# Regrouping the seven-product stages of a three-layer kernel: six groups of 768 tokens become four of 1024 and one of 512

## The chip, the core and the metric

The kernel runs on one core of one Trainium2 chip. The metric is the device time of one execution in microseconds (us); the time before is the median of three runs. A core has a matrix engine (TensorE, "PE" in the profile, with its weight loads in a row of their own, "PEld"), three elementwise engines (VectorE "DVE", ScalarE "ACT", GpSimd "POOL"), and SyncE ("SP"), whose queue issues most of the DMA transfers. Matrix products land in PSUM, which has eight banks; one bank holds 512 float32 columns. GpSimd works on SBUF tiles alone.

## The reference

```python
# attention inside chunks of 64 tokens: q, k, v are (8, 8, 576, 64)
scores = scale * np.matmul(q_c, k_c.transpose(0, 1, 2, 4, 3))
attn = softmax(scores)                          # with 1e-09 added to the sum
x = np.matmul(attn, v_c)                        # -> (4608 tokens, 512)
# first layer pair
gate = 1.0 / (1.0 + np.exp(-(x @ w_gate)))      # 512 -> 1536
y = (gate * (x @ w_val)) @ w_out                # 1536 -> 512
# second layer pair
h = y @ w_in                                    # 512 -> 2048
g = np.where(h >= 1, h, np.where(h <= -1, 0.0, (h + 1) ** 2 / 4))
out = g @ w_out2                                # 2048 -> 512
```

## The kernel before

The work is in four parts, one after the other.

- **Projection.** Nine blocks of 512 tokens go through attention and the two products of the first pair. The products are those of `proj_part`, named `pr` in the profile, with a moving operand of 512 columns. The eight first blocks hold the first 512 tokens of each of the eight batches; one more block, `REST`, holds the last 64 tokens of all eight. The gated result `sg` goes to DRAM (`gT`, `gR`). Beside this the weights of the later parts are combined and stored.
- **Stage o** (1536 to 512), **stage i** (512 to 2048) and **stage p** (2048 to 512). Each is a matrix product in blocks that uses seven half-size products instead of eight, numbered 1 to 7 and run in the order `PO = [1, 5, 6, 2, 7, 3, 4]`. A group of tokens is cut into two halves of `N` columns; the operand of a product is a quarter of the input (`b11` to `b22`) or a difference of quarters.

Each operand is split into a high part, rounded to the matrix engine's float32 format, and a low part, the remainder. So one block product takes three matrix instructions (`three`, lines 480 to 482: high by high, high by low, low by high). An operand is made in up to three steps, and here is who does each before the change:

- `op_sub` (line 525) subtracts two quarters, in place, for products 5, 6, 7 and 4: VectorE in o and p, GpSimd in most of i;
- `op_hi` (line 529) copies the high part: ScalarE;
- `op_lo` (line 536) subtracts the high part from the source: in o and p VectorE and GpSimd in turn, in i GpSimd.

A **step** is six matrix instructions. In `down` (stages o and p) it is one slice k of one product for both halves m of the output rows; in `up` (stage i) it is one product for one m, over both slices. The order on every engine is written out by step: `on(t, prio, fn, ...)` puts a piece of work ahead of step t. `op_sub` stands 8 steps, `op_hi` 7 and `op_lo` 6 ahead of the step that uses them. `result` (lines 551 and 553) takes a finished product out of its bank: ScalarE copies products 1, 6, 5 and 4, VectorE adds 2, 7 and 3 to what is already there. Products 1, 6, 7 and 4 pile up in one bank, of which there are two sets; line 543 takes them in turn by the parity of the group (in i of the output pair).

Behind stage i stands the function g. Before the change ScalarE forms relu(h/2 + 1/2), VectorE takes the minimum with 1 and squares in one instruction (`u_square`, line 715), and VectorE takes the maximum with h (`u_join`, line 720).

There are 6 groups of 768 tokens with N = 384, so 42, 56 and 56 steps for one group in o, i and p, and 5544 matrix instructions in the three stages. In p the operands lie in 10 tiles used in a ring (`p_tile`); the weights of a stage stay in SBUF for all groups. The output leaves through a 32 by 32 transpose on VectorE (`out_store`, line 786) and DMAs with rows of 128 bytes.

```python
eng = nc.vector if turn[0] % 2 == 0 else nc.gpsimd      # op_lo, line 535
i = (14 * (NG - 1) + np_[0] % 10) % NY                  # p_tile, line 770
n = 6 * par if BANK[p] == 0 else 2 * BANK[p]            # product, line 543
```

Of the kernel before, what the change touches and what calls it, by code (L numbers as in the profile page):

```python
# [30 lines left out]
def kernel(  # L31
# [29 lines left out]
    N = 384  # L61
    GT = 2 * N
    NG = NT // GT
    NR = 28
    PO = [1, 5, 6, 2, 7, 3, 4]

    wp = ctx.enter_context(tc.tile_pool(name="wp", bufs=NR))
    cp = ctx.enter_context(tc.tile_pool(name="cp", bufs=1))
# [5 lines left out]
    yT = [dp.tile([DM, GT], F32, name=f"yT{g}") for g in range(NG)]  # L74
    uT = [dp.tile([F2 * P, GT], F32, name=f"uT{g}") for g in range(NG)]

# [19 lines left out]
    def w_load(key):  # L96
        kind, f = key
        sl = slice(f * P, (f + 1) * P)
        if kind in "gv" and keys.index(key) < 8:
            raw = wp.tile([P, 512], I64, tag="w", name="raw")  # L100
        else:
            raw = pool["raw"].tile([P, 512], I64, tag="raw", name="raw", bufs=pool["nraw"])
# [58 lines left out]
    def s_split(kind, k, part):  # L161
# [9 lines left out]
        st = pool["raw"].tile([P, 2, 2, 256], F32R, tag="raw", name="st", bufs=pool["nraw"])  # L171
# [37 lines left out]
    pool = {}  # L209
    X = {}  # L210
# [9 lines left out]
    def x_tile(n=BS, name="x"):  # L220
        return pool["x"].tile([P, 2, n], F32R, tag="x", name=name, bufs=8)
# [11 lines left out]
    class Whole:  # L233
# [162 lines left out]
        def x(self, p):  # L396
            t = X[self.b, p] = x_tile()
            for r, b in enumerate(self.B["o", p]):
                nc.scalar.activation(self.half(t, 0, r), b, AF.Copy)

        def half(self, t, i, r):
            return t[:, i].rearrange("e (g r q) -> e g r q", r=2, q=CH)[:, :, r]

        def l(self, p):
            t = X[self.b, p]
            for r, b in enumerate(self.B.pop(("o", p))):
                nc.vector.tensor_tensor(
                    out=self.half(t, 1, r), in0=b, in1=f32(self.half(t, 0, r)), op=ALU.subtract
                )

    def first_block():
# [12 lines left out]
        z = pool["sg"].tile([P, BS], F32R, tag="sg", name="z", bufs=4)  # L424
# [82 lines left out]
    turn = [0]  # L507
# [3 lines left out]
    def quarters(p, key):  # L511
        b0, b1 = B0[key], B1.get(key)
        b21, b22 = (b1[:, :N], b1[:, N:]) if b1 is not None else (None, None)
        return b0[:, :N], b0[:, N:], b21, b22

# [11 lines left out]
    def op_hi(p, key, name, tile_):  # L527
        OP[name] = o = tile_()
        nc.scalar.activation(o[:, 0], op_src(p, key), AF.Copy)  # L529

    def op_lo(p, key, name, eng=None):
        o = OP[name]
        if eng is None:
            turn[0] += 1
            eng = nc.vector if turn[0] % 2 == 0 else nc.gpsimd
        eng.tensor_tensor(out=o[:, 1], in0=op_src(p, key), in1=f32(o[:, 0]), op=ALU.subtract)  # L536

    def product(p, m, pairs, par):

        for first, args in pairs:  # L540
            first = first and p in (1, 2, 5)
            if first:
                n = 6 * par if BANK[p] == 0 else 2 * BANK[p]
                banks[BANK[p], m] = ps.tile([P, N], F32, tag=f"b{n + m}", name=f"P{BANK[p]}")
# [22 lines left out]
    def down(kind, nk, tile_, load0, load1, done, first=0):  # L567
# [407 lines left out]
```

## Time and profile before

| | us |
|---|---|
| median of 3 runs | 1660.26 (1657.21 to 1660.83) |
| the profiled execution | 1659.88 |
| its span (first to last instruction of the program) | 1658.1 |
| TensorE busy | 1636.3 (99%) |
| VectorE busy | 1154.2 (70%) |
| ScalarE busy | 853.7 (51%) |
| GpSimd busy | 720.9 (43%) |

The span begins at 0. The projection ends and stage o begins at 687.64 us; stage i begins at about 950, stage p at about 1299; the last matrix instruction begins at 1653.61. A matrix instruction's duration in the profile is longer than the distance to the next one, since instructions overlap in the array; distances between starts are what counts for the total. The same holds for VectorE, where an instruction may start before the one ahead has fully ended: a row that joins two (x2) shows it.

### The profile page before, as it was taken

The numbers are of one execution on the slowest core, as the hardware profiler recorded it, in microseconds if no ns is written. First come the engines' busy times: TensorE is split into PE (matmuls) and PEld (weight loads), VectorE is DVE, ScalarE is ACT, GpSimd is POOL, SyncE is SP. The second block draws the span as 40 slices with busy tenths as digits, with TensorE's granted clock in tenths as the row PEclk, the third lists the DMA queues.
The fourth block names the chain that finished last, engine by engine and source line by source line (L and its number), as shares of the span: only waits on it lengthen the run. The fifth ranks groups of instructions, "written<-read, shape, count | busy, mean of one in ns | idle before, by whom it ended". The sixth has DMA issues, their size and how long they took to land.

```text
span 1658.1 us, 29812 instructions
## 1 busy us (share of the span) xinstructions
PE 1636.3 (99%) x10688; PEld 1512.4 (91%) x10688; DVE 1154.2 (70%) x1833; ACT 853.7 (51%) x1566; POOL 720.9 (43%) x666
## 2 busy tenths in 40 slices
PE   7999999999999999999999999999999999999999
PEld 6778888887888888899999999999999999999998
DVE  6865555555455531487777778788787899889887
ACT  6664445444554431355555565565554555555553
POOL 2433434343444420255555564353450555555553
PEclk9999999999999999999999999999999999999999
DMA  7957777777777858355744654423328844554462
GB/s 204 268 127 206 217 211 202 209 232 232 206 220 228 236 191 327 123 153 176 218 134 134 240 217 153 153 112 143 137 115 339 324 147 113 148 164 108 111 190 39
DMA packets 399844, 307.13 MB, mean 185 GB/s; under 512 B 275920, under 2 KB 322000, under 8 KB 399696
## 3 DMA queue, kind: packets, MB, share of 16 engines
q1 hardware_dynamic: 396496, 304.84, 59.8%
q8 instruction: 84, 1.38, 0.3%
q10 hardware_dynamic: 3200, 0.39, 0.1%
q14 instruction: 64, 0.52, 0.1%
HBM read 179.83 MB, written 125.30 MB: 184 GB/s over the span
## 4 chain that ended last, share of the span: by engine, by line
PE 88%; DVE 5%; DMA 2%; SPq 2%; ACT 1%; issue 1%; POOL 1%; POOLq 0%; DVEq 0%; ACTq 0%
PE P L481 18%; PE P L482 18%; PE P L480 18%; PE pr L480 10%; PE pr L482 10%; PE pr L481 10%; PE O L390 1%; DVE z L525 1%; SPq L298 1%; PE S L342 1%; PE PT L378 1%; DMA vd<-in_v_dram 1%; DVE raw L128 1%; SPq L287 1%; DVE z L536 1%
## 5 line engine op out<-in xcount | busy, mean ns | idle before, releaser
L481 PE MATMUL P<-z,w 128*128 128x384 f32 x1344 | 450.1, 335 | 2.4 <-DVE z L536 2.1
L482 PE MATMUL P<-z,w 128*128 128x384 f32 x1344 | 449.7, 335 | 0.0
L480 PE MATMUL P<-z,w 128*128 128x384 f32 x1344 | 449.6, 335 | 0.0
L536 POOL TENSOR_TENSOR z<-z 128x384 fp32r<-128x384 f32 x256 | 290.6, 1146 | 362.4 <-ACT z L529 355.1
L480 PE MATMUL pr<-x,w 128*128 128x512 f32 x864 | 344.6, 399 | 0.0
L482 PE MATMUL pr<-x,w 128*128 128x512 f32 x864 | 337.7, 391 | 0.7 <-POOL w L138 0.7
L481 PE MATMUL pr<-x,w 128*128 128x512 f32 x864 | 337.0, 390 | 0.0
L529 ACT ACTIVATE z<-z 128x384 fp32r<-128x384 f32 x420 | 211.6, 522 | 167.5 <-DVE z L525 71.7
L930 DVE TENSOR_TENSOR sg<-pr,sg 128x512 f32<-128x512 f32 x108 | 74.5, 689 | 286.9 <-PE pr L482 120.4
L481 PEld LDWEIGHTS P<-z,w 128*128 128x128 f32 x1344 | 252.8, 188 | 3.8 <-DVE z L536 3.1
L480 PEld LDWEIGHTS P<-z,w 128*128 128x128 f32 x1344 | 252.9, 188 | 0.0
L482 PEld LDWEIGHTS P<-z,w 128*128 128x128 f32 x1344 | 252.7, 188 | 0.0
L536 POOL TENSOR_TENSOR op<-in,op 128x384 fp32r<-128x384 f32 x126 | 142.1, 1133 | 197.1 <-ACT op L529 196.0
L482 PEld LDWEIGHTS pr<-x,w 128*128 128x128 f32 x864 | 162.4, 188 | 36.4 <-POOL w L138 1.5
L480 PEld LDWEIGHTS pr<-x,w 128*128 128x128 f32 x864 | 162.4, 188 | 34.0
L481 PEld LDWEIGHTS pr<-x,w 128*128 128x128 f32 x864 | 162.7, 188 | 31.8
L927 ACT ACTIVATE sg<-pr 128x512 f32<-128x512 f32 x108 | 64.5, 597 | 236.0 <-PE pr L482 224.6
L529 ACT ACTIVATE op<-in 128x384 fp32r<-128x384 f32 x252 | 128.5, 524 | 110.9 <-DVE in L525 53.8
L525 DVE TENSOR_TENSOR z<-z 128x384 f32<-128x384 f32 x198 | 179.2, 933 | 4.2 <-POOL z L536 4.0
L482 PE MATMUL P<-op,w 128*128 128x384 f32 x504 | 168.3, 334 | 0.0
L480 PE MATMUL P<-op,w 128*128 128x384 f32 x504 | 168.3, 334 | 0.0
L481 PE MATMUL P<-op,w 128*128 128x384 f32 x504 | 168.3, 334 | 0.0
(62 smaller groups left out, 2188.6 us busy)
## 6 DMA issues: line engine op xcount, KB each, us to landing
uT<-ua SPq DMA_DIRECT2D x96, 384.0 KB, 2.3
z<-uT SPq DMA_DIRECT2D x96, 384.0 KB, 5.9
gT<-sg SPq DMA_DIRECT2D x96, 256.0 KB, 4.6
in<-gT SPq DMA_DIRECT2D x48, 384.0 KB, 4.4
raw<-in_moe_w_out_dram SPq DMA_DIRECT2D x28, 512.0 KB, 5.8
w<-swi SPq DMA_DIRECT2D x28, 512.0 KB, 6.2
w<-swp SPq DMA_DIRECT2D x28, 512.0 KB, 7.1
swi<-st SPq DMA_DIRECT2D x24, 512.0 KB, 4.2
```

The costliest lines, as they stand in the source:

```text
L128: nc.vector.scalar_tensor_tensor(out=word(1, I32), in0=word(1, I32), scalar=3, in1=word(0, I32), op0=ALU.logical_shift_left, op1=ALU.bitwi ...
L287: nc.sync.dma_start(out=t[:, i, js, h], in_=rows[h ^ u].rearrange("(j i) d -> i j d", i=P)[:, js],)
L298: nc.sync.dma_start(out=t[32 * g:32 * g + 32, i, u * step // 32:(u + 1) * step // 32], in_=part.rearrange("(t i) r -> i t r", i=32),)
L342: nc.tensor.matmul(banks[h ^ u][hs, c], lhsT=t[rows, 0, ts], rhs=t[rows, 1, ts], start=True, stop=True)
L480: nc.tensor.matmul(o, lhsT=ah, rhs=bh, start=first, stop=False, skip_group_check=open_)
L481: nc.tensor.matmul(o, lhsT=ah, rhs=bl, start=False, stop=False, skip_group_check=open_)
L482: nc.tensor.matmul(o, lhsT=al, rhs=bh, start=False, stop=stop and last, skip_group_check=open_)
L525: (eng or nc.vector).tensor_tensor(out=op_src(p, key), in0=x, in1=y, op=ALU.subtract)
L529: nc.scalar.activation(o[:, 0], op_src(p, key), AF.Copy)
L536: eng.tensor_tensor(out=o[:, 1], in0=op_src(p, key), in1=f32(o[:, 0]), op=ALU.subtract)
L927: nc.scalar.activation(sg, go, AF.Sigmoid)
L930: nc.vector.tensor_tensor(out=sg, in0=vo, in1=sg, op=ALU.mult)
```

## The change

- **Groups.** N is 512 and a group has 1024 tokens: four groups (`FULL`) of two batches' first 512 tokens, and one (`REMNANT`) of the 512 tokens of the block `REST`, with halves of 256 columns. Stages o and i run them in the order 0, 1, remnant, 2, 3 (`AMID`); stage p runs 0 to 3 and then the remnant (`LAST`). The number of steps of a group stays, so the three stages have 4620 matrix instructions: 3696 with 512 columns and 924 with 256.
- **Memory.** One pool `wp` of 46 tiles of 4 KB takes the place of the pools for weights, raw weights, x, operands, inputs and outputs. Beside it are a pool of 7 tiles (`v`) for results and values of g, and one of 4 half tiles (`hp`). The remnant puts two slices into one tile (`part`). In p, of the operands after the 32nd, three of five go to the `v` pool.
- **Weights of stage i.** The 14 odd ones of 28 are loaded again for each group (`STREAM`), 16 steps ahead.
- **Low parts.** In o and p VectorE makes them all, but for the first product of p's first group; in i GpSimd goes on, but VectorE makes the operands (differences and low parts) of the group that follows the remnant.
- **The function g.** VectorE clips h to [-1, 1] (`tensor_scalar` with max and min), ScalarE forms the square of h/2 + 1/2, VectorE joins as before.
- **Output.** The four DMAs of a transposed tile are spread over steps instead of issued together, and all stand on SyncE's queue; the results of o and p are held in tiles of one half each.

```diff
-    N = 384
-    GT = 2 * N
-    NG = NT // GT
-    NR = 28
+    N = 512
+    FULL, REMNANT = NB // 2, NB // 2
+    NG = FULL + 1
+    AMID = [*range(FULL // 2), REMNANT, *range(FULL // 2, FULL)]
+    LAST = [*range(FULL), REMNANT]
+    NR = 46
+    def cols(g):
+        return N // 2 if g == REMNANT else N
...
+            if label == "op" and kind == "p":
+                turn[0] += 1
+                if turn[0] > VOP and turn[0] % 5 < 3:
+                    return v_tile(s, dt, label)
+            return wp.tile(s, dt, tag="w", name=label)
...
         if eng is None:
-            turn[0] += 1
-            eng = nc.vector if turn[0] % 2 == 0 else nc.gpsimd
+            eng = nc.vector
...
+    def clip(dst, src):
+        nc.vector.tensor_scalar(out=dst, in0=src, scalar1=-1.0, scalar2=1.0, op0=ALU.max, op1=ALU.min)
...
     def u_square(h, m):
         u = U[h, m]
-        nc.vector.scalar_tensor_tensor(out=u, in0=u, scalar=1.0, in1=u, op0=ALU.min, op1=ALU.mult)
+        nc.scalar.activation(u, u, AF.Square, scale=0.5, bias=half)
...
+    STREAM, AHEAD = {"i": range(1, 28, 2), "p": ()}, 16
```

VectorE in the last stage, a full group, while products 6 and 7 are made ready; `z` (before) and `op`, `u` (after) are operand and input tiles, L525 and L556 the differences, L536 and L566 the low parts. Before:

```order
L536 TENSOR_TENSOR z<-z 128x384
L525 TENSOR_TENSOR z<-z 128x384 x2
L536 TENSOR_TENSOR z<-z 128x384
L525 TENSOR_TENSOR z<-z 128x384 x2
L536 TENSOR_TENSOR z<-z 128x384
```

After:

```order
L566 TENSOR_TENSOR op<-u,op 128x512
L556 TENSOR_TENSOR u<-u 128x512
L566 TENSOR_TENSOR op<-u,op 128x512
L556 TENSOR_TENSOR u<-u 128x512
L566 TENSOR_TENSOR op<-u,op 128x512
```

One low part now goes with each difference, where one went with two.

VectorE in the middle stage, one pair of output rows m of a full group, from the last added result on; `R` are results, `P` the bank, `ua` the values of g. Before:

```order
L553 TENSOR_TENSOR R_12952<-P_12969,R_12952 128x384
L715 SCALAR_TENSOR_TENSOR ua<-ua 128x768
L720 TENSOR_TENSOR ua<-R_12937,ua 128x768
L715 SCALAR_TENSOR_TENSOR ua<-ua 128x768 x2
L720 TENSOR_TENSOR ua<-R_12952,ua 128x768
L720 TENSOR_TENSOR ua<-P_12930,ua 128x384
L720 TENSOR_TENSOR ua<-R_12964,ua 128x384
L715 SCALAR_TENSOR_TENSOR ua<-ua 128x768
```

After:

```order
L583 TENSOR_TENSOR R_11624<-P_11641,R_11624 128x512
L691 TENSOR_SCALAR ua<-R_11636 128x512
L691 TENSOR_SCALAR ua<-R_11609 128x1024
L691 TENSOR_SCALAR ua<-P_11602 128x512
L691 TENSOR_SCALAR ua<-R_11648 128x512
L691 TENSOR_SCALAR ua<-R_11624 128x1024
L691 TENSOR_SCALAR ua<-P_11617 128x512
L717 TENSOR_TENSOR ua<-R_11609,ua 128x1024
L717 TENSOR_TENSOR ua<-R_11624,ua 128x1024
```

The squares have left VectorE, and clips of one source have come, all ahead of the joins.

TensorE where stage o turns into stage i, with what each instruction waits for; `P0` are banks (the number tells them apart), `op` and `z` operands, `w` weights. Before:

```order
L481 MATMUL P0_9680<-op_10053,w_7251 128x384 [waits DVE_49]
L482 MATMUL P0_9680<-op_10053,w_7251 128x384
L480 MATMUL P0_9684<-op_10053,w_7251 128x384
L481 MATMUL P0_9684<-op_10053,w_7251 128x384
L482 MATMUL P0_9684<-op_10053,w_7251 128x384
L480 MATMUL P0_10160<-z_10082,w_8304 128x384 [waits DMAHW5_49,Activation_49]
```

After:

```order
L494 MATMUL P0_9161<-op_9546,w_7231 128x512 [waits DVE_49]
L495 MATMUL P0_9161<-op_9546,w_7231 128x512
L493 MATMUL P0_9165<-op_9546,w_7231 128x512
L494 MATMUL P0_9165<-op_9546,w_7231 128x512
L495 MATMUL P0_9165<-op_9546,w_7231 128x512
L493 MATMUL P0_9636<-op_9575,w_8699 128x512 [waits DMAHW5_49,Activation_49]
```

The last row is the first product of stage i. Its wait for ScalarE was for its operand alone. By the parity of line 543 the last group of o, the fifth in the order now and the sixth before, has the set of banks that i's first pair takes (P0_9161 and P0_9636 are one bank), so the wait now covers ScalarE's copy out of P0_9161 too, whose last product ended four instructions earlier.

## Rows read from the trace of the kernel before

**Rows 1.** The page: span, busy time by engine, the chain that ended last.
```profile
span 1658.1 us, 29812 instructions
PE 1636.3 (99%) x10688; PEld 1512.4 (91%) x10688; DVE 1154.2 (70%) x1833; ACT 853.7 (51%) x1566; POOL 720.9 (43%) x666
PE 88%; DVE 5%; DMA 2%; SPq 2%; ACT 1%; issue 1%; POOL 1%; POOLq 0%; DVEq 0%; ACTq 0%
```

**Rows 2.** Timeline, TensorE (start, length): 28 instructions of 512 columns, 25 of 384.
```profile
640.04 0.39 PE L480 MATMUL pr<-x,w 128*128 128x512 f32 x1
...
646.16 0.39 PE L480 MATMUL pr<-x,w 128*128 128x512 f32 x1
...
999.67 0.33 PE L480 MATMUL P<-z,w 128*128 128x384 f32 x1
...
1003.83 0.33 PE L480 MATMUL P<-z,w 128*128 128x384 f32 x1
```

**Rows 3.** Timeline, weight loads and matrix instructions behind a break in the projection.
```profile
301.36 0.19 PEld L480 LDWEIGHTS pr<-x,w 128*128 128x128 f32 x1
301.47 0.19 PEld L481 LDWEIGHTS pr<-x,w 128*128 128x128 f32 x1
...
301.36 0.50 PE L480 MATMUL pr<-x,w 128*128 128x512 f32 x1
301.70 0.39 PE L481 MATMUL pr<-x,w 128*128 128x512 f32 x1
```

**Rows 4.** Timeline, TensorE: first and last instruction of the three stages.
```profile
687.64 0.33 PE L480 MATMUL P<-op,w 128*128 128x384 f32 x1
...
1653.61 0.34 PE L482 MATMUL P<-z,w 128*128 128x384 f32 x1
1653.98 0.58 DVE L786 STREAM_TRANSPOSE RT<-P 128x384 f32<-128x384 f32 x1 [3.58 <-PE P L482]
```

**Rows 5.** Stretches where stage p begins: busy us (and instructions), granted clock, DMA.
```profile
1250.00:1308.00 58.00, 57.84 (x334) 57.52 (x332) 44.26 (x61) 28.63 (x52) 13.84 (x11) 1.00 0.91 343
1307.00:1316.00 9.00, 7.18 (x31) 6.55 (x31) 8.97 (x14) 3.46 (x8) 3.68 (x4) 0.81 0.91 344
```

**Rows 6.** Timeline there: two waits of TensorE, and VectorE between them.
```profile
1308.16 0.44 PE L481 MATMUL P<-z,w 128*128 128x384 f32 x1 [0.32 <-POOL z L536]
1309.90 0.55 DVE L525 TENSOR_TENSOR z<-z 128x384 f32<-128x384 f32 x1
1310.37 0.55 DVE L536 TENSOR_TENSOR z<-z 128x384 fp32r<-128x384 f32 x1
1310.97 0.46 PE L481 MATMUL P<-z,w 128*128 128x384 f32 x1 [1.50 <-DVE z L536]
```

**Rows 7.** Stage p by line: duration ns min/median/max; GpSimd makes 159 low parts beside these.
```profile
L536 DVE TENSOR_TENSOR z<-z x157: 507/546/1386, 1314.8 to 1639.1; 128x384 fp32r<-128x384 f32 x157
L525 DVE TENSOR_TENSOR z<-z x184: 508/890/1408, 1315.3 to 1638.6; 128x384 f32<-128x384 f32 x184
```

**Rows 8.** Timeline, VectorE: two instructions in a row, of 256 and of 512 columns.
```profile
101.38 0.75 DVE L407 TENSOR_TENSOR x<-O,x 128x256 fp32r<-128x256 f32 x2
135.97 1.28 DVE L128 SCALAR_TENSOR_TENSOR raw<-raw 128x512 int32<-128x512 int32 x2
```

**Rows 9.** Groups by line and shape (count, busy us, mean ns): 256 and 512 columns.
```profile
L407 DVE TENSOR_TENSOR x<-O,x 128x256 fp32r<-128x256 f32 x72 | 26.9, 415 | 4.1 <-ACT x L399 4.0
L930 DVE TENSOR_TENSOR sg<-pr,sg 128x512 f32<-128x512 f32 x108 | 74.5, 689 | 286.9 <-PE pr L482 120.4 <-issue 106.9 <-ACT st L172 37.5
L927 ACT ACTIVATE sg<-pr 128x512 f32<-128x512 f32 x108 | 64.5, 597 | 236.0 <-PE pr L482 224.6 <-DMA in<-gT 4.8 <-DMA qk<-in_q_dram 2.9
L172 ACT ACTIVATE st<-raw 128x512 fp32r<-128x512 f32 x66 | 41.4, 664 | 13.4 <-POOL raw L151 6.8 <-POOL raw L153 5.3 <-DMA swp<-st 1.3
```

**Rows 10.** Stretches of stages i and p: VectorE busy is the third number.
```profile
960.00:1290.00 330.00, 330.00 (x1905) 330.00 (x1904) 267.89 (x363) 183.90 (x343) 128.18 (x111) 1.00 0.46 175
1315.00:1640.00 325.00, 324.44 (x1870) 323.64 (x1869) 295.14 (x415) 177.16 (x364) 179.08 (x159) 1.00 0.48 139
```

## What the change was predicted to do

> **What bounds the kernel now.** First the page: TensorE is busy 99% of the span and holds 88% of the chain that ended last, VectorE 5% [rows 1]. Then TensorE's first and last instruction of the three stages: 687.64 to 1653.61 and one more distance, 966.1 us [rows 4]. The change leaves the projection's work as it is, so the whole argument is about these 966.1 us. Two things can shorten them: less time from start to start, and fewer waits.
>
> The distance from start to start comes from the timeline [rows 2]. In stretches without a wait, 24 distances of 384 columns take 1003.83 - 999.67 = 4.16 us, 0.1733 each; 27 of 512 columns take 646.16 - 640.04 = 6.12 us, 0.2267 each. The 128 columns between them cost 0.0534, the clock's upper level (2.4 GHz); the granted clock of stages i and p is 1.00 [rows 10]. So an instruction pays 4 x 0.0534 for 512 columns and 0.0131 whatever its size. The columns of all instructions together stay (5544 x 384 = 3696 x 512 + 924 x 256), so fixed parts are all that the new sizes save.
>
> The waits: 5544 x 0.1733 = 960.8, so all waits before come to 966.1 - 960.8 = 5.3 us. They stand where stage p begins: from 1307 to 1316 TensorE starts 31 instructions where about 52 would fit, at a granted clock of 0.81, and VectorE is busy 8.97 of the 9 us [rows 5]. The instruction rows there say "POOL" for one wait and VectorE for a longer one of 1.50 us, with VectorE going from a difference to a low part between them [rows 6].
>
> **Instructions.** After the change 3696 x 0.2267 = 837.9. For 256 columns no row of this kind of stream exists. Bounds: not under the spacing of the weight loads when nothing holds them, 301.47 - 301.36 = 0.11 [rows 3], as each instruction loads new weights; not over 0.1733, the row of 384. The line through the two rows gives 0.1733 - 0.0534 = 0.1199, just over the lower end, and I take it: 924 x 0.1199 = 110.8. Sum 948.7, against 960.8: **-12.1 us**. Bounds from the 256-column rows: -21 to +37.
>
> The Trainium skill, page "TensorE: Matmul & The Clock Gate", section "Wait — 56ns, not 53.3ns?", says of back-to-back matmuls that a warm one costs N / 2.4 GHz and about 2.5 ns. By that the instructions would take 900.9 us before and 898.5 after, and the saving would be 2.4. The trace disagrees at both sizes: 0.1733 and 0.2267 [rows 2] are some 10 ns longer than its 0.1625 and 0.2158. It stands beside rival (c).
>
> **VectorE's load, the cover of it all.** Durations of 512 columns are 0.69 and of 256 columns 0.415 [rows 9], but two in a row take 1.28 and 0.75 [rows 8], so the next starts after about 0.60 and 0.33. A full group of p lasts 56 steps x 6 x 0.2267 = 76.2 us, the small one 40.3. VectorE has in it 56 low parts, 32 differences, 6 added results and 8 transposes, 102 instructions: 61 us by spacing, 70 by duration; small group 34 and 42. It fits in a full group either way; the small one fits by spacing only. Stage o: 72 instructions, 43 of 57.1 us; small 24 to 30, of 30.2. Stage i: GpSimd keeps differences and low parts. VectorE loses the squares and gets clips; clips, joins and added results of a full group come to about 45 of 76.2 us, against 268 in 330 us (81%) before [rows 10]. The group behind the small one has its 22 operand instructions on VectorE instead, some 7 us during the small group: 32 of 40.
>
> These are VectorE's times without company. In stage p before, its 415 instructions took 295.14 us, 0.71 each [rows 10], while the shortest difference took 0.508 and the median one 0.890 [rows 7]. GpSimd was at work in the same stretch for 179 us. Low parts, median 0.546, suffered little. I read the excess as GpSimd's company at the differences; after the change GpSimd is idle in o and p, and the excess goes. That reading is not shown by a row, and rival (b) is its failure.
>
> In p, operands come out of a shared pool: with 28 weights and 16 inputs of 46 tiles taken, 2 remain, and 3 of the `v` pool's 7: five tiles where there was a ring of ten. A high part then waits for the product five steps ahead of its own; four steps (5.4 us) remain for high part, 0.66, and low part, 0.69 [rows 9], and for what VectorE has in front of it, at most two results and two transposes, 2.7 us. That is covered; in the small group all of it halves.
>
> **ScalarE** gives up 144 relu instructions and takes the squares, 64 of 1024 columns in full groups. At 0.66 for 512 it is busy about 40 of 76 us in i, and hidden. If it weren't, the join and then the store behind it would be late, not TensorE, as results leave their banks before.
>
> **Waits.** The old 5.3 us at p's start go: VectorE was full there with squares, joins and differences, and the squares have left. What is late next is GpSimd, which makes the first product's eight low parts and two differences of the second. At 179.08 / 159 = 1.13 for 384 columns [rows 10], 1.5 for 512 (scaled), ten are 15 us, in a product of 8 steps x 1.36 = 10.9 us with a lead of six steps, 8.2. It fits with 4 us to spare; one late input uses that up. I take **2**, bounds 0 and 5.3 (the old wait).
>
> New is the wait where o turns into i: the bank of i's first product is the one that o's last group just filled, so TensorE waits for ScalarE's copy, 0.60 [rows 9], which starts when the last product has left the array, 0.39 - 0.23 = 0.16 after its slot [rows 2]; three other instructions run meanwhile, 0.68. So 0.60 + 0.16 - 0.68 = 0.1 and the semaphores; one other ScalarE instruction in front adds 0.66. I take **0.5**, bounds 0.1 and 0.8. Queued behind that copy on ScalarE are the second copy and the operand copies of i, which lie steps ahead.
>
> Inside the small group's three stretches TensorE may wait for a low part. I take **0.5**, bounds 0 and 8 (rival (a)). Together +3.
>
> **The end.** Behind the last product stand one transposition and its DMAs, 1653.61 to 1658.1 [rows 1, 4]. The transposition of 256 columns is shorter (0.58 to 0.415); the four DMAs now follow each other on one queue. Bounds -0.2 and +2; I take **+0.3**, as the transfers still run together.
>
> **DMA.** In the last group of stage i some 52 transfers of 512 KB are issued (stores, p's weights and inputs): 27.3 MB in 76.2 us is 358 GB/s. The densest stretch shown moved 343 at 91% busy [rows 5]; at that rate they last 79.5, 3 us longer. The loads have many steps of lead, so nothing now; rival (e).
>
> **Sum.** 1659.88 - 12.1 - 5.3 + 3 + 0.3 = 1645.8 on the profiled execution's scale; the median stands 0.38 above that execution: **1646**. The bounds of the turn, the bank and the end give -2.9 to +5.3, distances of 0.115 to 0.122 at 256 columns -4.5 to +2; as not all ends come together, the forecast's own range is 1641 to 1653.
>
> **Rivals.**
> (a) *The small groups aren't fed.* If VectorE goes by full durations, it needs 42 us where the small group of p has 40.3; bursts then make TensorE wait, and after a wait it ran at 0.81 in [rows 5]. Price: 2 in i, 2 to 4 in p, 2 in o, and a few for the clock: 1655 to 1660. For it: the rows with x2 are few. Against: o and i have their small group in the middle, where lead is large.
> (b) *Slower: VectorE becomes the bound of stage p.* If the excess of 0.20 per instruction (0.71 against 0.508) isn't GpSimd's doing, an instruction of 512 takes 0.60 + 0.20 = 0.80, a full group 102 x 0.80 = 81.6 against 76.2, four times +5.4; the last group 102 x 0.53 = 54 against 40.3, +14. In all +36, so 1682. It starts at a mean of 76.2 / 102 = 0.75 and makes the whole slower than before from about 0.79. For it: VectorE was at 91% in p with GpSimd's help, and now has that share too. Against: the low parts' median of 0.546 in the same stretch.
> (c) *The instruction term is nothing*: the fixed part of 13 ns belongs to the two stretches that I looked at, one in the projection and one in i, and elsewhere columns alone count. Without the 12.1 the sum is 1658. Against: the same three code lines issue both, and 5544 x 0.1733 leaves just the waits that the rows show. The rule of the Trainium skill's page "TensorE: Matmul & The Clock Gate" tends this way; its 2.4 would give 1656.
> (d) *256 columns cost as much as 384*, 0.1733: 924 x 0.053 = +49, so 1695. Against: loads alone go at 0.11 [rows 3].
> (e) *DMA bounds the last group of i*: 3 to 8 us, 1650 to 1655.
> (f) *The wait at the turn to p stays* as it was, since the late one is GpSimd, as the first row names: 1651. Then the squares' move didn't do what it seems to.
>
> **How the numbers follow.** Forecast 0.63, (a) 0.14, (b) 0.10, (c) 0.03, (d) 0.02, (e) 0.05, (f) 0.03. A measurement of this kernel tells about 0.2%, 3.3 us: faster is under 1656.9, slower over 1663.6. Faster: the forecast, (e), (f) and the lower two fifths of (a), 0.77. Slower: (b) and (d), 0.12. Same: (c) and the rest of (a), 0.11. The range from 1641 to 1661 leaves out (b), (d) and a little of the forecast's lower side, and takes in (a), (c), (e) and (f).
>
> **What would show it.** Starts 0.2267 apart in full groups and 0.120 in small ones. In p, differences and low parts of full groups with nearly the same median, about 0.69; a median over 0.8 there, VectorE near 100% and TensorE waiting for low parts is (b). No wait over a microsecond where p begins; if there is one, the releaser tells (f) from the old cause. One wait of half a microsecond at the first product of i, released by ScalarE. Waits in the small groups, and a granted clock under 1.00 there, are (a). Over 343 GB/s and waits for weights or inputs late in i are (e).

## The result, and the profile after

The median of the changed kernel is 1645.83 us (five runs, 1644.93 to 1648.8) against 1660.32 of the kernel before: a ratio of 0.9919, 95% interval 0.9906 to 0.9932. The prediction said 1646. The profiled execution has a span of 1644.6, against 1658.1. The page after, its span, its busy times and the chain that ended last (as [rows 1]):

```profile
span 1644.6 us, 26890 instructions
PE 1622.7 (99%) x9764; PEld 1354.6 (82%) x9764; DVE 1091.8 (66%) x1947; ACT 803.4 (49%) x1350; POOL 351.8 (21%) x332
PE 90%; DVE 3%; SPq 2%; DMA 2%; ACT 1%; issue 1%; POOL 0%; DVEq 0%; ACTq 0%
```

TensorE was the bound and still is. GpSimd lost half of its work, and VectorE, which took over low parts, is busy for less time than before. Why VectorE does more in less time is one thing that the experiments have to explain.

The timeline of TensorE after (start, length), as [rows 2] and [rows 4]: the first instruction of stage o, two of 512 columns, two of 256, and the last one.

```profile
687.25 0.39 PE L493 MATMUL P<-op,w 128*128 128x512 f32 x1
...
1499.81 0.39 PE L493 MATMUL P<-op,w 128*128 128x512 f32 x1
...
1501.17 0.39 PE L493 MATMUL P<-op,w 128*128 128x512 f32 x1
...
1620.00 0.28 PE L493 MATMUL P<-op,w 128*128 128x256 f32 x1
...
1620.72 0.28 PE L493 MATMUL P<-op,w 128*128 128x256 f32 x1
...
1638.60 0.28 PE L495 MATMUL P<-op,w 128*128 128x256 f32 x1
```

Six distances of 512 columns are 1.36 us, 0.2267 each; six of 256 are 0.72, 0.120 each. From the first start to the last the three stages take 951.35 us, against 965.97 [rows 4]. 3696 x 0.2267 + 924 x 0.120 is 948.7, so all waits together are 2.7 us. In the kernel before they were 5.4 in the same count, which takes all time over the instructions at full clock for waits; 1.6 of the 5.4 turn out below to be something else.

The difference of the two spans, -13.5 us, falls into four parts:

| | us |
|---|---|
| instructions of the three stages, 960.60 to 948.64 | -11.96 |
| waits in them (all other time), 5.36 to 2.71 | -2.65 |
| from the last matrix instruction's start to the end, 4.48 to 5.95 | +1.47 |
| start of stage o, 687.64 to 687.25 | -0.39 |

**Where the 2.7 us of waits are.** 0.3 stands at the first product of i, whose weight load waits for ScalarE's copy. The rest, 2.4, stands in the small group of stage i, behind ScalarE. The weight load first, then TensorE in the small group (in brackets the idle time before the instruction and what released it):

```profile
946.16 0.19 PEld L493 LDWEIGHTS P<-op,w 128*128 128x128 f32 x1 [0.43 <-ACT R L581]
...
1101.88 0.39 PE L493 MATMUL P<-op,w 128*128 128x256 f32 x1 [0.21 <-ACT R L581]
...
1103.71 0.39 PE L493 MATMUL P<-op,w 128*128 128x256 f32 x1 [0.85 <-ACT R L581]
```

And ScalarE in the same stretch:

```profile
1099.37 2.19 ACT L712 ACTIVATE ua<-ua,half 128x1024 f32<-128x1024 f32 x2 [0.43 <-DVE ua L691]
1101.46 0.36 ACT L581 ACTIVATE R<-P 128x256 f32<-128x256 f32 x1
1101.73 1.14 ACT L712 ACTIVATE ua<-ua,half 128x1024 f32<-128x1024 f32 x1
1102.77 0.62 ACT L560 ACTIVATE op<-y 128x512 fp32r<-128x512 f32 x1
1103.29 1.19 ACT L581 ACTIVATE R<-P 128x256 f32<-128x256 f32 x4
```

L712 is the square, still of the full group ahead with 1024 columns; L581 copies product 1 of the small group out of its bank. Product 6 piles up on that bank and can't start before the copy. A step of the small group lasts 0.72 us, and a square of the large one 1.1. The two waits shown cost 1.6 of the 2.4 us, the longer distance behind each included; the rest are several short ones up to 1135 us, too short for the trace to name a releaser.

**Where p begins** there is no wait, where [rows 6] had two. VectorE ends its joins (L717) and goes to the low parts (L566) and differences of p:

```profile
1301.58 1.17 DVE L717 TENSOR_TENSOR ua<-R,ua 128x512 f32<-128x512 f32 x1
1302.68 0.68 DVE L566 TENSOR_TENSOR op<-u,op 128x512 fp32r<-128x512 f32 x1
1303.28 0.68 DVE L556 TENSOR_TENSOR u<-u 128x512 f32<-128x512 f32 x1
```

**Stage p** from 1320 to 1600 us, VectorE being the third number with its count of instructions, GpSimd the fifth. Before:

```profile
1320.00:1600.00 280.00, 279.44 (x1610) 278.64 (x1609) 252.27 (x360) 150.94 (x310) 153.14 (x137) 1.00 0.51 147
```

After:

```profile
1320.00:1600.00 280.00, 280.00 (x1243) 232.09 (x1243) 233.02 (x378) 140.73 (x239) 0.00 (x0) 1.00 0.50 147
```

VectorE runs 378 longer instructions in less time than 360 shorter ones, 0.616 us each. Low parts and differences by line there:

```profile
L566 DVE TENSOR_TENSOR op<-u,op 128x512 fp32r<-128x512 f32 x202 | 137.2, 686 | 44.5 <-ACT op L560 41.7
L556 DVE TENSOR_TENSOR u<-u 128x512 f32<-128x512 f32 x112 | 76.8, 685 | 0.0
```

### The profile page after: what moved, and what is told of

The parts are those of the page before. It is cut to its first block, busy times and chain, and to the rows that moved or that the text cites. A ratio compares the mean times of both kernels' runs of the same rounds, so it can differ in the third digit from the quotient of the medians.

```text
span 1644.6 us, 26890 instructions
## 1 busy us (share of the span) xinstructions
PE 1622.7 (99%) x9764; PEld 1354.6 (82%) x9764; DVE 1091.8 (66%) x1947; ACT 803.4 (49%) x1350; POOL 351.8 (21%) x332
## 4 chain that ended last, share of the span: by engine, by line
PE 90%; DVE 3%; SPq 2%; DMA 2%; ACT 1%; issue 1%; POOL 0%; DVEq 0%; ACTq 0%
PE P L493 19%; PE P L495 19%; PE P L494 19%; PE pr L493 10%; PE pr L495 10%; PE pr L494 10%; SPq L306 1%; PE O L398 1%; PE S L350 1%; PE PT L386 1%; DMA vd<-in_v_dram 1%; DVE raw L132 1%; DVE raw L124 1%; DMA qk<-in_k_dram 0%; ACT raw L128 0%
## 5 line engine op out<-in xcount | busy, mean ns | idle before, releaser
L493 PE MATMUL P<-op,w 128*128 128x512 f32 (+1 forms) x1540 | 567.3, 368 | 1.1 <-ACT R L581 1.1
L494 PE MATMUL P<-op,w 128*128 128x512 f32 (+1 forms) x1540 | 566.4, 368 | 0.0
L495 PE MATMUL P<-op,w 128*128 128x512 f32 (+1 forms) x1540 | 566.4, 368 | 0.0
L493 PEld LDWEIGHTS P<-op,w 128*128 128x128 f32 x1540 | 290.3, 188 | 50.7 <-ACT R L581 2.2
L494 PEld LDWEIGHTS P<-op,w 128*128 128x128 f32 x1540 | 290.3, 189 | 48.1
L495 PEld LDWEIGHTS P<-op,w 128*128 128x128 f32 x1540 | 290.3, 189 | 47.9
L560 ACT ACTIVATE op<-u 128x512 fp32r<-128x512 f32 (+1 forms) x280 | 158.7, 587 | 160.1 <-PE P L495 86.0
L583 DVE TENSOR_TENSOR R<-P,R 128x512 f32<-128x512 f32 (+1 forms) x180 | 114.4, 637 | 131.2 <-PE P L495 130.5
L566 DVE TENSOR_TENSOR op<-u,op 128x512 fp32r<-128x512 f32 (+1 forms) x272 | 168.7, 630 | 48.4 <-ACT op L560 45.3
L566 POOL TENSOR_TENSOR op<-y,op 128x512 fp32r<-128x512 f32 (+1 forms) x56 | 67.5, 1221 | 513.0 <-DMA w<-swi 330.3
L560 ACT ACTIVATE op<-in 128x512 fp32r<-128x512 f32 (+1 forms) x210 | 116.5, 585 | 91.9 <-DVE in L556 56.3
L712 ACT ACTIVATE ua<-ua,half 128x1024 f32<-128x1024 f32 (+1 forms) x80 | 82.9, 1060 | 131.2 <-DVE ua L691 130.0
L566 DVE TENSOR_TENSOR op<-in,op 128x512 fp32r<-128x512 f32 (+1 forms) x210 | 128.3, 639 | 22.8 <-ACT op L560 22.3
L581 ACT ACTIVATE R<-P 128x512 f32<-128x512 f32 (+1 forms) x198 | 105.1, 549 | 49.4 <-PE P L495 48.9
```

The lines of the kernel that those rows point to most:

```text
L493: nc.tensor.matmul(o, lhsT=ah, rhs=bh, start=first, stop=False, skip_group_check=open_)
L494: nc.tensor.matmul(o, lhsT=ah, rhs=bl, start=False, stop=False, skip_group_check=open_)
L495: nc.tensor.matmul(o, lhsT=al, rhs=bh, start=False, stop=stop and last, skip_group_check=open_)
L581: nc.scalar.activation(r(i), b, AF.Copy)
L583: nc.vector.tensor_tensor(out=r(i), in0=b, in1=r(i), op=ALU.add)
L712: nc.scalar.activation(u, u, AF.Square, scale=0.5, bias=half)
```

## The experiments

The three stages are timed within a trace, from their first matrix instruction to the start of the last, since the work ahead of them scatters (last run of this section). "Waits" is that time less the instructions at 0.2267 (512 columns), 0.1733 (384) and 0.120 (256). The quarters and a second trace of the changed kernel stand in the text.

| kernel | median us | three stages | waits |
|---|---|---|---|
| before | 1659.0 to 1660.3 | 965.96 | 5.4 |
| before, squares on ScalarE | 1657.06 | 963.02 | 2.4 |
| before, low parts on VectorE | 1655.66 | 962.62 | 2.0 |
| before, both | 1655.61 | 960.81 | 0.2 |
| changed | 1645.83 | 951.35 | 2.7 |
| changed, squares on VectorE | 1652.36 | 956.32 | 7.7 |
| changed, low parts in turn | 1650.11 | 954.16 | 5.5 |
| changed, three repairs | 1645.51 | 949.09 | 0.5 |
| changed, repairs, other queues | 1642.47 | 949.08 | 0.4 |
| changed, quarter twice | 1646.6 | 952.12 | 3.5 |
| changed, half twice | 1669.93 | 974.47 | 25.8 |
| changed, halves in p | 1663.68 | 967.59 | 3.3 |

### What took the old wait away: squares or low parts

Two theories stood against each other. A: VectorE's squares made the wait at p's start. B: it came from the low parts, shared between VectorE and GpSimd. Four kernels undo or do one of the two edits, and a fifth does both.

**Squares back on VectorE, in the changed kernel.**

```diff
 def clip(dst, src):
-    nc.vector.tensor_scalar(out=dst, in0=src, scalar1=-1.0, scalar2=1.0, op0=ALU.max, op1=ALU.min)
+    nc.scalar.activation(dst, src, AF.Relu, scale=0.5, bias=half)
...
 def u_square(h, m):
     u = U[h, m]
-    nc.scalar.activation(u, u, AF.Square, scale=0.5, bias=half)
+    nc.vector.scalar_tensor_tensor(out=u, in0=u, scalar=1.0, in1=u, op0=ALU.min, op1=ALU.mult)
```

> The changed kernel with the function g made as before: relu on ScalarE, minimum and square in one instruction on VectorE. Theory A (the squares on VectorE made the wait where stage p begins): VectorE gets three squares of 1024 columns, about 6 us, between the last product of i and its first difference of p, and loses about 3 us of clips; a wait of 1 to 4 us comes back within the first 12 us of p. The waits of the small group in i (2.2 us, behind ScalarE's squares) go. In all 1644 to 1649 us. Rival B (the wait came from VectorE and GpSimd sharing the low parts, or from the six groups): no wait at p's start, and without the small group's 2.2 the time is 1643.6 us.

Measured: 1652.36 us (ratio to before 0.9956, 0.994 to 0.9973), 5.0 us more in the three stages. TensorE's waits, summed by releaser:

```profile
PE P L493 <- ACT R L581: 2.3, 2, 1.5
PE P L494 <- DVE op L566: 1.9, 1, 1.9
PE P L493 <- DVE R L583: 1.8, 1, 1.8
```

The second row is the wait at p's start, and VectorE shows it coming:

```profile
1304.07 2.31 DVE L712 SCALAR_TENSOR_TENSOR ua<-ua 128x1024 f32<-128x1024 f32 x1
1306.41 0.69 DVE L717 TENSOR_TENSOR ua<-P,ua 128x512 f32<-128x512 f32 x1
1307.02 0.68 DVE L717 TENSOR_TENSOR ua<-R,ua 128x512 f32<-128x512 f32 x1
1307.62 0.68 DVE L566 TENSOR_TENSOR op<-u,op 128x512 fp32r<-128x512 f32 x1
```

The first low part begins 14.8 us after the last added result of i (1292.79), instead of 11.4 (1291.32 to 1302.68). The last square takes 2.31 us there, where the median of this run's squares is 1.22; GpSimd is at work on p's operands until 1305.3, so its company may be part of it, which no run separates. A holds for this wait. The rest of the expectation failed: the waits in and ahead of the small group didn't go but grew from 2.4 to 5.2, since VectorE, with squares, is now the one that is late there. The third row says so, and behind the first row, ScalarE's copies, VectorE stands too: ScalarE's queue had waited for VectorE's differences just before.

```profile
1088.80 0.63 ACT L560 ACTIVATE op<-y 128x512 fp32r<-128x512 f32 x1 [5.35 <-DVE y L556]
...
1117.70 0.63 ACT L560 ACTIVATE op<-y 128x512 fp32r<-128x512 f32 x1 [2.31 <-DVE y L556]
```

**Low parts in turn again, in the changed kernel.**

```diff
         if eng is None:
-            eng = nc.vector
+            low[0] += 1
+            eng = nc.vector if low[0] % 2 == 0 else nc.gpsimd
```

> The changed kernel with the low parts of o and p made by VectorE and GpSimd in turn, as before. Theory A (GpSimd's company lengthens VectorE's differences): the differences of p's full groups go from a median of 0.684 us to about 1.19 (0.890 x 512 / 384), those made by GpSimd take 1.3 us or more; VectorE's sum per full group is about 32 x 1.1 + 28 x 0.65 + 14 x 0.65 = 63 of 76 us, so TensorE has no new wait and the time stays within 3 us of 1645.8. Theory B (the low parts on VectorE are what took the old wait at p's start away): a wait of 2 to 5 us at p's start, 1648 to 1651 us.

Measured: 1650.11 us (0.9941, 0.9926 to 0.9956), 2.8 us more in the three stages, as waits of TensorE for low parts of VectorE in p; the end behind the last product is 7.4 us long instead of 5.95. Stage p, the same stretch, and VectorE by line:

```profile
1320.00:1600.00 280.00, 279.52 (x1238) 230.64 (x1237) 231.30 (x276) 141.32 (x241) 154.06 (x106) 1.00 0.50 145
...
L557 DVE TENSOR_TENSOR u<-u 128x512 f32<-128x512 f32 x114 | 123.4, 1108 | 0.0
L568 DVE TENSOR_TENSOR op<-u,op 128x512 fp32r<-128x512 f32 x102 | 83.0, 819 | 45.8 <-ACT op L561 44.7 <-POOL op L568 0.9
...
L585 DVE TENSOR_TENSOR R<-P,R 128x512 f32<-128x512 f32 x24 | 15.7, 679 | 0.0
```

GpSimd took 106 low parts, VectorE ran 276 instructions instead of 378, and was busy 231.3 us instead of 233.0. A difference went from 0.685 to 1.108, near the expected 1.19. The added results, which read one operand from PSUM, kept their 0.68. The part of the expectation that saw no new wait failed: a low part that VectorE itself makes is now late now and then.

**Squares to ScalarE, in the kernel before.**

```diff
 def u_relu(h, m):
...
-    nc.scalar.activation(dst, src, AF.Relu, scale=0.5, bias=half)
+    nc.vector.tensor_scalar(out=dst, in0=src, scalar1=-1.0, scalar2=1.0, op0=ALU.max, op1=ALU.min)
...
 def u_square(h, m):
     u = U[h, m]
-    nc.vector.scalar_tensor_tensor(out=u, in0=u, scalar=1.0, in1=u, op0=ALU.min, op1=ALU.mult)
+    nc.scalar.activation(u, u, AF.Square, scale=0.5, bias=half)
```

(and a clip for the relu of product 4, too.)

> The kernel before with the new function g alone: clip on VectorE, square on ScalarE. Theory A (squares): the waits at p's start, 4.7 us by 1349 us, shrink to under 1 us, and the time falls by 4 to 5 us to about 1656. Theory B (low parts, differences): the waits stay, 1659 to 1661 us.

Measured: 1657.06 us (0.9984, 0.9974 to 0.9993). In the three stages, 2.9 us less. The waits between 1300 and 1325 us fell from 3.9 to 0.7, as A says; those from 1325 on stayed, 1.6 after 1.2. So the time fell by less than A expected. Of the 3.9, 1.6 were no waiting (see the run with both).

**Low parts to VectorE, in the kernel before.**

```diff
-            turn[0] += 1
-            eng = nc.vector if turn[0] % 2 == 0 else nc.gpsimd
+            eng = nc.vector
```

> The kernel before with all low parts of o and p on VectorE. Theory A (squares made the wait at p's start): the wait stays at 2 us or more, 1657 to 1661 us; the differences in p fall from a median of 0.890 us to about 0.51, and VectorE's sum in p stays about the same, near 290 of 325 us, although it makes twice the low parts. Theory B (the sharing of low parts made it): no wait, 1655 to 1656 us. Rival (b) of the prediction (VectorE becomes the bound of p when it makes all low parts): TensorE waits for low parts all through p, 1665 us or more.

Measured: 1655.66 us (0.9977, 0.9968 to 0.9986). One wait of 1.7 us at p's start is left, and none later. It stands where the longer wait of [rows 6] stood, and is as long (1.51 after 1.50 us of idle time):

```profile
1310.57 0.44 PE L481 MATMUL P<-z,w 128*128 128x384 f32 x1 [1.51 <-DVE z L535]
```

So the low parts didn't make that wait: it went with the squares, in the run ahead of this one, and it comes back with them in the changed kernel. Stage p:

```profile
1320.00:1600.00 280.00, 280.00 (x1618) 280.00 (x1616) 237.03 (x497) 154.29 (x312) 0.00 (x0) 1.00 0.53 151
...
L535 DVE TENSOR_TENSOR z<-z 128x384 fp32r<-128x384 f32 x273 | 145.4, 549 | 29.2 <-ACT z L529 29.0
L525 DVE TENSOR_TENSOR z<-z 128x384 f32<-128x384 f32 x154 | 85.1, 553 | 2.7 <-DMA z<-uT 2.6
```

VectorE makes 137 instructions more than in the kernel before and is busy 15 us less (237.03 after 252.27). Rival (b) of the prediction is refuted here.

**Both, in the kernel before.**

> The kernel before with both: the squares on ScalarE with clips on VectorE, and all low parts of o and p on VectorE. If the waits of the kernel before came from VectorE's squares at the turn and from GpSimd's company, none over 0.3 us is left: the three stages take 960.6 to 961.3 us (966.0 before), 1655 us. What the groups and tiles then bring is 961 - 951.35 = 9.6 us, the instruction term of -12.0 less the new waits of 2.7. Rival: the wait at 1345 to 1350 us stays, 962 us or more.

Measured: 1655.61 us (0.9977, 0.9968 to 0.9986); 960.81 us for the three stages, 0.2 of waits. Of 5.4 us the squares alone take away 3.0, the low parts alone 3.4, both 5.2. But 1.6 of the 5.4 were no waiting: in the trace of the kernel before, eleven distances behind the wait of 1.50 us, from 1311.26 to 1314.73, take 3.47 us instead of 1.91, at a granted clock of 0.50, the lower of the two levels (1.2 GHz):

```profile
1311.88 0.52 PE L481 MATMUL P<-z,w 128*128 128x384 f32 x1
...
1313.80 0.52 PE L481 MATMUL P<-z,w 128*128 128x384 f32 x1
```

(Six distances in 1.92 us.) In the traces of the edited kernels the clock is 1.00 throughout the three stages, behind waits of 1.51 and 1.85 us at the same place too. So these 1.6 us come from a single trace, and no run shows which edit, if either, took them away. Without them the squares carry the wait of 1.50 us, and the low parts the 1.2 us from 1325 on; the short first wait of [rows 6] went with either. Neither theory was the whole. What the new groups and tiles bring is then 960.81 - 951.35 = 9.5 us: 12.0 of instructions less 2.5 of new waits.

### The instruction term

**Halves in stage p.** In `product`, for p's full groups and k > 0:

```diff
+            if cut:
+                ah, al, bh, bl = args
+                for c in (slice(0, 256), slice(256, 512)):
+                    three(banks[BANK[p], m][:, c], [(ah, al, bh[:, c], bl[:, c])], start=False, open_=True)
+                continue
```

> The changed kernel where in p's full groups each matrix instruction of 512 columns, but for the first slice of a product, is cut into two of 256 columns: 1176 instructions more, the same columns. If an instruction costs 13.3 ns whatever its size (0.2267 and 0.120 us from start to start), +15.6 us, 1661.4 us. If it costs 2.5 ns, +2.9, 1648.7 us. If a weight load for each instruction bounds the stream at 256 columns, more than +16.

Measured: 1663.68 us (1.0023, 1.0014 to 1.0032). The three stages are 16.2 us longer than the changed kernel's, for 1176 more instructions: 13.8 ns each, or 13.3 without the 0.6 us of it that are waits. The columns are the same, so that is what an instruction with a weight load of its own, as all have here, costs beyond its columns. Whether the price is the load's or the instruction's, no run separates.

**Quarters**, the same with four slices of 128 columns.

> As the run with halves, each matrix instruction of 512 columns in p's full groups, but for a product's first slice, cut into four of 128. By the line (0.0131 and 0.0534 for 128 columns) four take 0.266 us, +0.039 for each of 1176, +46 us against the changed kernel. If the weight loads, 0.11 us apart, bound the stream: four take 0.44, +0.213 each, +251 us, 1897 us.

Measured: 1906.61 us in one run; the three stages take 1210.7, 259 us more. TensorE in p, matrix instructions:

```profile
1499.76 0.28 PE L493 MATMUL P<-op,w 128*128 128x128 f32 x1
1499.87 0.27 PE L494 MATMUL P<-op,w 128*128 128x128 f32 x1
...
1500.43 0.28 PE L493 MATMUL P<-op,w 128*128 128x128 f32 x1
```

and their weight loads:

```profile
1499.81 0.19 PEld L494 LDWEIGHTS P<-op,w 128*128 128x128 f32 x1
1499.92 0.19 PEld L495 LDWEIGHTS P<-op,w 128*128 128x128 f32 x1
```

Six distances take 0.67 us, 0.112 each, the pace of the loads, as the second case of the expectation has it. At 128 columns the line (0.067) no longer holds; at 256 it does, with 0.120 just over the loads' pace.

### How far VectorE is from being the bound

In p's full groups a quarter, and then half, of the low parts are made twice, in `op_lo`; the half:

```diff
         eng.tensor_tensor(out=o[:, 1], in0=op_src(p, key), in1=f32(o[:, 0]), op=ALU.subtract)
+        if key[0] == "p" and key[1] != REMNANT and eng is nc.vector and key[2] % 2 == 1:
+            eng.tensor_tensor(out=o[:, 1], in0=op_src(p, key), in1=f32(o[:, 0]), op=ALU.subtract)
```

> The changed kernel with a quarter of the low parts of p's full groups made twice on VectorE (14 more instructions of 512 columns for one group, 116 instead of 102). If VectorE's cost is its spacing, 0.60 us, it needs 70 of 76.2 us: no wait, 1645 to 1648 us. If it is the duration, 0.685: 79.5 us, +3.3 for each of four groups, about 1659 us.

> As the run before, with half of the low parts made twice (28 more, 130 for one group). By spacing, 0.60 us: 78 of 76.2 us, VectorE is the bound by 1.8 us for each group, about +8, 1654 us, with TensorE waiting for low parts. By duration, 0.685: 89 us, +13 for each group, about +51, 1697 us.

Measured: a quarter 1646.6 us (0.9928, 0.9911 to 0.9946), with 0.8 us more in the three stages, half 1669.93 (1.0069, 1.0052 to 1.0086). Stage p with half of them twice:

```profile
1320.00:1600.00 280.00, 272.81 (x1149) 211.88 (x1149) 276.09 (x445) 131.57 (x222) 0.00 (x0) 1.00 0.44 129
```

276.09 / 445 is 0.620 us for each, with VectorE busy 99%. So spacing, not duration, is the cost, 0.62 rather than 0.60, and 76.2 us hold some 123 instructions; the changed kernel has 102 in a full group. At 130 the excess was 23 us in all instead of the 8 expected. The wait of 0.87 us for the same low part comes back every 81.9 us (1353.04, 1434.87, 1516.78, 1598.70): VectorE is then the bound at 0.63 for each of 130 instructions, idle time included, and 5.7 us over 76.2, four times, are nearly the whole excess.

### Repairs of what the change left behind

```diff
-                        steps.append((up_step, g, jj % 2, jj, p, m))
+                        steps.append((up_step, g, (jj + 1) % 2, jj, p, m))
+                        late = int(REMNANT in (g, AMID[min(gi + (jj + 1) // NJ, NG - 1)]))
...
-                            on(t + 2, 2, u_square, 1, m)
-                            on(t + 3, 2, u_join, 1, m)
+                            on(t + 2 + late, 2, u_square, 1, m)
+                            on(t + 3 + late, 2, u_join, 1, m)
...
-        eng = nc.sync
+        eng = nc.scalar if last and c in (1, 2) and a % 2 else nc.sync
```

(and the other parity in p's banks, too.)

> The changed kernel with three small repairs: the banks of i and p taken in the other turn, so that i's first product doesn't take the bank that o's last group has just filled; in i, ahead of and within the small group, the squares and joins of the second half one step later, behind ScalarE's copy of the next pair's first product; at the end, half of the last transfers on ScalarE's queue, as before. Each wait has its own place, so one trace shows all three. Expected: the wait of 0.28 us at i's first product goes to 0; of the small group's 2.25 us in i 0.5 to 1.2 remain; the stretch from the last product to the end of the span falls from 5.9 us to about 4.7. In all -2.5 us, about 1643.3. Rival: the small group's copies are late for the first half's squares too, and nothing changes there; 1644.3.

Measured: 1645.51 us (0.9917, 0.9902 to 0.9931). The wait at i's first product is gone, 0.5 us of the small group's are left, and the three stages take 949.09, 2.3 less. The end stayed at 5.9 us, so that part of the expectation failed. In the traces a transfer waits for the landing of the one eight ahead of it, even on the other queue. SyncE's run of transfers begins at 1638.60, as one of ScalarE's queue lands (1638.58):

```profile
1638.60 4.01 SPq L792 DMA_DIRECT2D out_dram<-RT  x7
```

In the changed kernel itself, the last transposition and SyncE's queue:

```profile
1638.92 0.45 DVE L775 STREAM_TRANSPOSE RT<-P 128x256 f32<-128x256 f32 x1 [2.42 <-PE P L495]
...
1637.93 4.39 SPq L790 DMA_DIRECT2D out_dram<-RT  x9
```

Nine issues in 4.39 us are 0.49 each; the last four begin at about 1640.4, a microsecond after the transposition has ended, as the queue is still at work on the tiles ahead.

**Another sharing of the last transfers**, with the other two repairs:

```diff
+        eng = nc.scalar if last and (c == 1 or c == 2 and m == 1 and a % 2) else nc.sync
```

> The changed kernel with the repairs of the banks and of the small group's squares, and the last transfers shared out in another way: the eight of product 3 on ScalarE's queue, the first four of product 4 on SyncE's, the last four half on each. If the end is long because sixteen transfers stand on one queue at 0.49 us each (the last four begin 1.1 us after their tile is transposed), they begin at once and the end falls from 5.95 to 4 us; with 949.1 us for the three stages the whole is 4.2 us shorter than the changed kernel from the same start of stage o, 1641.7 by the median if the starts are alike. If the end is set by how long a transfer takes to land: 5.5 us or more.

Measured: 1642.47 us (0.9906, 0.989 to 0.9921), and from the last matrix instruction to the end 4.2 us. Its last transposition ends at 1636.45, and the issues of both queues are through by 1637.7:

```profile
1636.00 0.45 DVE L777 STREAM_TRANSPOSE RT<-P 128x256 f32<-128x256 f32 x1 [2.43 <-PE P L495]
...
1633.60 4.07 SPq L792 DMA_DIRECT2D out_dram<-RT  x6
...
1632.62 4.69 ACTq L792 DMA_DIRECT2D out_dram<-RT  x8
```

This is the fastest kernel of the study, 4 us under the changed one by the next run: 2.3 of it in the three stages, 1.7 to 1.9 at the end.

**The changed kernel again**, measured together with that one.

> The changed kernel as it is, on the same chip as the next run and the same runs of before, for the scatter of the unchanged projection: stage o has begun between 684.5 and 691.5 us in the traces so far, though its work ahead of that is the same in all. Expected: the three stages take 951.35 us again, within 0.3, and the start of o differs from 687.25 by a few us; 1643 to 1650 us.

Measured: 1646.46 us (0.9928, 0.9915 to 0.994). The three stages take 951.36 us, against 951.35 in the first trace, while o's start moved from 687.25 to 688.21. Over all fourteen traces it lies between 684.5 and 691.5. So a median tells little below 2 or 3 us for this kernel, and the stretch within the trace tells hundredths.

## Why the prediction was right

**The instruction term** was right in its number and its cause. It said 948.7 us at 0.2267 and 0.1199; the trace has 0.2267 and 0.120. Rival (c) falls with the halves in p: 13.8 ns for an instruction. The Trainium skill's page "TensorE: Matmul & The Clock Gate" (section "Wait — 56ns, not 53.3ns?") has about 2.5 ns for back-to-back matmuls; the measurement differs, and decides for this kernel. Rival (d) falls with the rows above.

**VectorE's cover** was right. The spacing of 0.60 from [rows 8] is 0.62 in the trace, and the reading that GpSimd's company made the excess of [rows 7] is now shown in both directions (a difference of 512 columns from 0.685 to 1.108 when it comes back, one of 384 from a median of 0.890 to a mean of 0.553 when it goes). Rival (b) fell on that. In stage i, where GpSimd goes on, VectorE was busy for 53 us of a full group's 76.2 instead of the 45 forecast; TensorE had no wait for it. The Trainium skill, page "SBUF — State Buffer", section "SBUF: two separate sides", names a port pair that VectorE and GpSimd share and that one of them holds for a whole instruction; a VectorE instruction with two SBUF inputs takes it. The traces agree: differences and low parts, with two such inputs, were lengthened, the added results from PSUM were not (0.679).

**The waits** came to 2.7 us where 3 was predicted, but by offsetting errors; each step on its own:

- *The start of p*: 2 predicted, 0 measured. GpSimd's part there, eight low parts and two differences of 1.3 to 2.3 us, 15.2 in all where 15 were forecast, was over at 1302.2, in time. What the prediction gave as the cause of the old 5.3 us, the squares, holds for the wait of 1.50 alone. It put all 5.3 at p's start and called them waits; 1.2 stood later in p and went with the low parts, and 1.6 were the lower clock, which it had before it as the mean of 0.81 in [rows 5]. So the term came out right for three reasons, of which it gave one.
- *The bank at i's first product*: 0.5 predicted, 0.3 measured, released by ScalarE as it said, and gone with the other parity.
- *The small group*: 0.5 predicted, for low parts, in any of the stages; 2.4 measured, in i alone, behind ScalarE. The step that failed is the one on ScalarE: "the join and then the store behind it would be late, not TensorE, as results leave their banks before". Results leave by copies on ScalarE itself, and those queue behind the squares. ScalarE's total was hidden; its order wasn't. Rival (a) looked at the right group and the wrong engine, and its own condition, VectorE by full durations, didn't occur. That the squares' place was the cause is shown by the repairs: a step later, ahead of and within the small group, 0.5 us are left.

**The end** was mis-sized: +0.3 predicted, +1.5 measured. The prediction counted the four last transfers on one queue and not the twelve ahead of them, which still stood there.

**DMA**, rival (e): 343 GB/s was no bound. From 1215 to 1300 us the DMA engines were busy 0.89 of the time, at 348 GB/s on average, and TensorE had no wait:

```profile
1215.00:1300.00 85.00, 85.00 (x377) 70.38 (x376) 56.32 (x83) 39.51 (x53) 12.83 (x9) 1.00 0.89 348
```

Rival (f) fell as well: no wait at the turn to p, and with the low parts alone on VectorE the old wait stayed, with VectorE named.

The sum's errors were -2.0 and -0.2 at the two turns, +1.9 in the small group, +1.2 at the end and -0.4 at the start of o. They leave +0.5: the profiled execution took 1646.35, the sum on its scale was 1645.8. Without that luck the range would still have held: with the positive errors alone the sum would be off by 3.1, with the negative ones alone by 2.6. A hit to 0.2 us was no merit of the waits' sizes.

## What to carry to other kernels

Cost a stream of matrix instructions by its distances from start to start at two sizes: the slope is the clock, the rest a price for each instruction, and larger tiles save just that. Before calling the remaining time waits, read the granted clock there: nearly a third of the old ones was a slower clock. Before sharing elementwise work between VectorE and GpSimd, look at VectorE's durations with and without GpSimd at work; here one engine alone did all of it in less time. An engine with spare time can still be the one that is waited for, wherever its long instructions of one group stand ahead of short copies that free a bank for the next.

## What the runs showed of the hardware

- A low part on GpSimd cost VectorE at least as much as making it. In the kernel before, 137 on GpSimd with 360 instructions on VectorE kept VectorE busy for 252 us; all 497 on VectorE alone took 237.
- The price of a matrix instruction that loads its own weights is, beyond its columns, 13 to 14 ns down to 256 columns; at 128 the weight loads, 0.112 us apart, set the pace.
- In the changed kernel's last run of nine, transfers left one queue 0.49 us apart, and on two queues they can still wait for each other's landing (issue at 1638.60, landing at 1638.58).
- The clock fell to 0.50 for 3.4 us behind a wait of 1.50 us in the kernel before; behind one of 1.51 and one of 1.85 us at the same place in two edited kernels it stayed at 1.00.
- The projection's length scattered by 7 us over fourteen traces whose work up to stage o is nearly or wholly the same, the three stages by 0.01 us in two runs of one kernel. Why the projection does so was not looked into.
